# A gated mix of a spectral filter and a Mish MLP on one core: loads of the filter weights moved to GpSimd's queue, the gate row spread by a matmul, another opening and another order of tasks

## The chip, the core and the metric

The kernel runs on one core of a Trainium2 chip. A core has five engines with instruction streams of their own: TensorE (PE; its weight loads are shown apart as PEld), VectorE (DVE), ScalarE (ACT), GpSimd (POOL) and SyncE (SP). They meet only at semaphores. Transfers between the chip's memory (HBM) and the core's SBUF are put into queues by an engine and carried out by 16 DMA engines that all queues share. Matmuls write to PSUM, which has eight banks of 128 x 512 f32.

The metric is device time in microseconds of one execution. The profile is of one such execution; its span is the time from the first to the last recorded instruction, a little under the device time of that execution.

## The reference: what is computed

```python
x = A_x                                          # [1, 2048, 512] bf16
g = sigmoid((x * gate_w).sum(-1, keepdims=True)) # one gate per row of x
# branch A: a filter in the frequency domain
X = rfft2(x, axes=(-2, -1))                      # 2048 x 257 complex
a = irfft2(X * (w_r + 1j * w_i))                 # W = w_r + i w_i: [2048, 257]
# branch B: an MLP on another input name, 512 -> 1792 -> 512, activation Mish
h = x @ w1 + b1
b = (h * tanh(softplus(h))) @ w2
return g * a + (1 - g) * b
```

The kernel as it stands takes x for both branches.

## The kernel before, in words

The 2048 rows of x are 16 tiles of 128 rows; for the MLP four tiles make a chunk (0 to 3).

- MLP, first layer: tasks `m{chunk}_{ft}`, for 14 blocks of 128 hidden columns, four matmuls of 512 columns each (line 847), and ACT's Mish `h{chunk}_{ft}` (line 852) into `hs`. In chunk 0 the blocks 0 to 3 are cut into two halves of two matmuls, `ma0_ft` and `m0_ft`, because w1's first columns come in two transfers, `w1_0_0` and `w1_0_2`. Blocks 8 to 10 need `w1_8_0`. Second layer: `n{tile}_0`, 14 matmuls (line 865), then `o{tile}_0`, which scales by 1 - g.
- The MLP needs x transposed. Tiles 0 to 3 are transposed on PE (`tr0` to `tr3`, line 573) and copied out by `evx0` to `evx3` on ACT or DVE; tiles 4 to 15 by transposing DMAs (`xt4` to `xt15`) in SP's queue, four to a chunk.
- Spectral branch: DVE makes sums and differences of x's halves (`bf`, line 586), PE the stages `p` (line 604), `d` (line 619) and `t0` to `t3` (line 698, with constants `ldM0` to `ldM3`), each followed by a copy out of PSUM (`ep`, `ed`, `et`) on ACT or DVE. Then DVE multiplies by the spectral weights (`hp`, `p1`, `ad`, lines 717 to 724), with a small correction through PE (`e1`, `e2`, then `e3` on DVE, line 767). The way back is `it` (line 780), `id` (line 819) and `ip` (lines 873, 888) on PE.
- The spectral weights W arrive as ten loads into a staging tile `rS` (`wr0s0` and so on, named matrix, half, part; three parts for half 0, two for half 1). DVE and ACT copy them into place: `wrm`/`wim` (lines 646 to 649), the duplicate `wrn`/`win` (line 661).
- The gate: `graw` loads the row `gate_w` copied to all 128 partitions, `gt0` to `gt15` (line 593) on DVE multiply and sum a tile of x with it, `zcl` clips, `ez` (line 681) is a power on POOL, the exponential; from it come `omg` (1 - g), `gc` (g), and, by `ezb`, the PE transpose `zt`, the copy `zte` and the transfers `zw` and `zr` through HBM, a row form of the exponential that `rfs` needs late.

Nothing is scheduled at run time. One string, `ORDER`, lists all tasks; each engine runs its own tasks in that order and stands still until the one at its head has its semaphores, even if a later one could go. A suffix gives the engine and the PSUM bank or slot of `tmp`: `evx2:dve`, `m0_8::7`. Durations written in the code (`pe()`, `dve()`) do nothing at run time.

Three rules of `place` matter. A task that takes a PSUM bank waits for the last users of that bank. A load in SP's queue waits for the landing of the sixth load before it, so that at most six are under way (`KOUT`, lines 268 to 275); this counts only loads in SP's queue. A computing task on POOL waits for the DVE task last marked `lock` ahead of it in the string (lines 261 to 267); DMAs on POOL don't.

The W loads also wait for x, for `cFD` (the constants of `d`) and for w1's first four transfers to land (`deps=t_fr`, line 557). `warm` is matmuls on ones that nobody reads, ahead of the first data; `fl0` and `fl1` are one more each.

Of the kernel before, what the change touches and what calls it, by code (L numbers as in the profile page):

```python
# [8 lines left out]
BF = mybir.dt.bfloat16  # L9
# [6 lines left out]
NFT = 14  # L16
NCH = 4
NF = 64
NFILL = 2
KOUT = 6  # L20
XTP = 4
W1P = ((0, 2, 0, 4), (2, 4, 0, 4), (0, 4, 4, 8), (0, 4, 8, 11), (0, 4, 11, 14))
# [304 lines left out]


ORDER = """
warm::0 fl0::1 fl1::2 ones ident x1 bf1_1 x0 bf0_0 bf0_1 x3 bf3_1 bf3_0 tr1::3 cRF braw evx1:act tr_b::4 x2 bf1_0 w1_0_0 bf2_1 w1_0_2 w1_8_0 ev_b  # L330
bf2_0 tr0::5 tr3::6 p0::0 tr2::7 evx2:dve p1 ep0:dve x4 p2::2 p3 evx3:act w1_4_0 x12 evx0:act ma0_0::4 ma0_2::6 graw::0 ma0_1::5 m0_1 tab w1_11_0 x8
h0_1 m0_2 xt4 xt7 ep2:dve h0_2 xt5 m0_8::7 h0_8 bf4_1 ma0_3::0 bf4_0 m0_3 m0_9::1 h0_9 m0_0 xt6 h0_0 cFD p6::2 h0_3 p7 ep6:dve bf12_0 ldM0 m0_7::5
h0_7 wi0s0 bf12_1 gt12 m0_4::6 h0_4 p4::0 m0_6::7 p5 h0_6 gt14 wi0s2 p14::3 ep4:act m0_10::2 gt13 p12::5 p15 ep14:act ebase m0_5::7 gt5 gt7 h0_10 h0_5
p13 bf8_0 ep12:act bf8_1 gt11 m0_13::0 h0_13 m0_11::1 h0_11 wi0s1 m0_12::3 h0_12 p8::6 p9 ep8:act xt10 gt1 p10::4 p11 ep10:dve m1_9::2 h1_9 wr0s2
m1_12::0 d8::6 d9 xt15 h1_12 xt8 gt8 ed8:act d0::4 d12::2 d13 xt11 ed12:act gt4 xt9 gt9 xt13 gt10 ldM1 wr0s0 m1_4::1 d1 ed0:act wr0s1 d4::6 d5 ed4:act
xt14 m1_13::0 m1_2::2 h1_4 wi1s0 d10::4 d11 ed10:act h1_2 wi1s1 ldM2 d2::6 gt0 d3 m1_8::3 h1_8 m1_5::1 h1_5 gt2 d14::4 gt6 gt15 gt3 zcl d15 ed14:act
wim010:dve m1_3::2 h1_3 ed2:dve m1_10::3 xt12 h1_10 wim011:dve wim000:dve wim001:dve wic0:dve t0::64 d6::1 ez win0:dve h1_13 d7 wr1s0 et00:act
et01:dve wr1s1 m1_0::3 wiz0 hp01_1::1 hp00_1::2 ed6:act m2_2::0 h2_2 hp00_0 h1_0 hp01_0 w2_10 m2_7::6 h2_7 t1::41 et10:act et11:act hp11_0::0 m2_10::7
hp11_1 h2_10 ldM3 m1_1::0 w2_0 m2_5::3 h2_5 wrm000:act m2_0::6 wrm011:dve wrm010:dve ldG2 wrm001:dve wrc0:act c01 m1_7::4 wrn0:dve wrz0 ez1 omg c00
p1_01 m2_9::5 p1_00 m1_6::1 h1_6 h2_0 wim100:dve h1_1 wim101:dve m2_6::2 ad_01 hp10_1::1 m2_3::7 w2_5 ldG0 m2_1::3 h2_1 h2_3 m2_4::1 h2_4 wim111:dve  # L340
m2_11::6 h2_11 hp10_0 h2_6 p1_11 m2_8::0 m1_11::3 h2_8 wim110:dve h2_9 t2::61 et20:act m3_2::0 m2_12::5 m3_6::6 et21:act ad_11 h2_12 m3_1::7 m3_7::1
m2_13::2 p1_10 wic1:act h1_11 wrm111:dve h1_7 wrm101:act wrm100:dve h2_13 m3_12::5 wrm110:dve wrc1:act h3_1 h3_2 m3_0::3 ad_10 wrn1:dve edge ldG1 h3_6
m3_10::4 win1:dve wiz1 ldG3 m3_11::2 h3_11 m3_13::7 h3_0 h3_13 h3_12 wrz1 c02 m3_8::0 hp20_0::0 h3_10 hp20_1 m3_5::6 hp21_0::1 h3_7 m3_9::2 m3_3::3
h3_9 m3_4::7 h3_4 ad_00 hp21_1 p1_21 t3::41 ad_21 et30:act hp30_0::2 n3_0::7 et31:act c03 hp30_1 p1_30 p1_20 h3_3 e1::4 ad_30 xp20::1 h3_8 o3_0:act
ad_20 h3_5 n2_0::5 n0_0::1 xp1::2 xp21 ead::0 e2::2 o0_0:act hp31_1::1 hp31_0 n1_0::3 o1_0:act p1_31 ad_31 rft e3 it5_0::6 it2_0::0 it2_1 it5_1 inv
eit5:act n5_0::4 o5_0:act ezb zt::2 eit2:dve it1_0::0 o2_0:dve it1_1 zte it0_0::6 it0_1 eit0:act zw zr eit1:act it3_0::2 it3_1 eit3:dve n6_0::5
it4_0::6 it4_1 it7_0::3 it7_1 o6_0:dve it6_0::1 it6_1 eit6:act n9_0::0 rfs eit4:dve eit7:act id0::1 id14::6 id15 ec14:act:2 ey14_1 id1 ec0:act:0
id2::4 id3 ec2:act:1 ey0_0 n7_0::3 ey14_0 ey2_0 id10::6 id11 ey2_1 o7_0:act ey0_1 id8::4 id9 ec8:dve:2 ey8_1 id6::1 ec10:act:1 ey10_0 n4_0::3 o4_0:act
ey8_0 ip9_0 ey10_1 id12::4 id7 id13 ec12:dve:0 ey12_1 id4::6 id5 ec4:dve:2 ec6:act:1 n8_0::3 ip8_0 ey6_1 o9_0:act ey6_0 n10_0::0 o8_0:act ey4_0 ip1::1
ey12_0 gc ey4_1 ip5::2 ip4::4 fin4 ip2::5 ip0::3 fin5 ip10_0 fin2 n13_0::6 n14_0::7 ip14_0 ip13_0 out9 n11_0::4 ip11_0 o11_0:act ip6::2 o10_0:dve  # L350
out11 ip7::5 out5 fin1 o14_0:dve fin0 out1 ip3::0 out14 n12_0::1 ip12_0 fin3 n15_0::7 ip15_0 fin6 fin7 o13_0:dve out7 out3 o12_0:dve out13
o15_0:act out15:act
"""


def _build(nc, A_x, A_w_r, A_w_i, B_x, B_w1, B_b1, B_w2, gate_w, out, merge=8, xtp=XTP, NWARM=8):
    cs = _build_consts()
    d_front = nc.inline_tensor(_bf16_bits(cs["front"]), name="c_front").bitcast(BF)
    d_inv = nc.inline_tensor(_bf16_bits(cs["inv"]), name="c_inv").bitcast(BF)
# [7 lines left out]
    with es:  # L367
# [62 lines left out]
        def bank(b, i=0):  # L430
            return ps[:, b.slot + i, :]
# [29 lines left out]
        def dma(name, dst, src, us, cls="dma", queue="sp", is_out=False, transpose=False, grp=None, **kw):  # L461
            def fn(e, _dst=dst, _src=src):
                a = _dst() if callable(_dst) else _dst
                b = _src() if callable(_src) else _src
                if transpose:
                    return e.dma_start(a, b, transpose=True)
                return e.dma_start(a, b)  # L467
# [40 lines left out]


        one = nc.const_aps.tensor(1.0, [128, 128], BF)  # L510
        one2 = nc.const_aps.tensor(1.0, [128, 256], BF)
        wb = _Buf("b1")

        def f_warm(e):
            ins = None
            for _ in range(NWARM):
                ins = e.matmul(bank(wb)[:, 0:256], one, one2, start=True, stop=True)
            return ins

        G.add("warm", [("pe", NWARM * 0.213, f_warm)], "warm", writes=[wb])  # L520
        for k in range(NFILL):
            fb = _Buf("b1")

            def f_fill(e, fb=fb):
                return e.matmul(bank(fb)[:, 0:256], one, one2, start=True, stop=True)
# [21 lines left out]
        for ri, (src, nm) in enumerate(((A_w_r, "wr"), (A_w_i, "wi"))):  # L547
            wv = src.rearrange("(q m) k -> q m k", m=128)
            for fh in range(2):
                sg = stg[64 * ri + 32 * fh:64 * ri + 32 * fh + 32]  # L550
                c0_ = 1 - fh
                parts = [(0, slice(0, 32), slice(32 * fh, 32 * fh + 32), 1.2),
                         (1, slice(c0_, 32), slice(127, 96, -1) if fh == 0 else slice(96, 64, -1), 1.75)]
                if fh == 0:
                    parts.append((1, slice(0, 1), slice(64, 65), 0.1))
                for j, (pm, fs, ms, us) in enumerate(parts):
                    dma(f"{nm}{fh}s{j}", sg[pm:32:2, fs, :], wv[:, ms, :], us, writes=[(nm, fh, "s", j)], deps=t_fr, grp=f"{nm}{fh}")
        for t in range(xtp, NT):
            dma(f"xt{t}", xT[:, t // 4, :, t % 4, :], xv[:, t, :], 0.55, transpose=True, writes=[("xT", t)], grp=f"xt{t // 4}")

# [21 lines left out]
        for a, b_ in XP:  # L582
            w = b_ - a
            for uv in range(2):
                def f_bf(e, a=a, b_=b_, uv=uv):
                    return e.tensor_tensor(out=xu[:, a:b_, uv, :], in0=x_sb[:, a:b_, 0:256], in1=x_sb[:, a:b_, 256:512],  # L586
                                           op=ALU.add if uv == 0 else ALU.subtract)

                t_bf.append(G.add(f"bf{a}_{uv}", [("dve", dve2(256 * w), f_bf)], "bf", lock=True,
                                  reads=[("x", t) for t in range(a, b_)], writes=[("xu", uv, t) for t in range(a, b_)]))  # L590
        t_gt = []
        for t in range(NT):
            t_gt.append(G.add(f"gt{t}", [("dve", 0.6, lambda e, t=t: e.scalar_tensor_tensor(  # L593
# [356 lines left out]
```

## Time and profile before

| | us |
|---|---|
| median of three runs (lowest, highest) | 131.74 (131.31, 131.85) |
| the profiled execution's own time | 131.67 |
| its span | 130.1 |
| PE busy in the span | 124.7 |
| DVE busy | 92.8 |
| ACT busy | 74.0 |
| POOL busy | 4.7 |

A row of a timeline has the start in us, the time from the start to the end of the last one, the engine, the line, the operation, out<-in, the shape, the count, and in brackets the idle time ahead of it with what ended it. Matmuls overlap, so a row of n takes n steps and the length of the last one. SPq and ACTq are the issuing of DMAs, which is not their moving of data; "us to landing" is.

### The profile page before, as it was taken

Reading aid. Unit: us, or ns where it says so; the run is one execution under the profiler, and the core shown is the slowest. Engines: PE = TensorE matmul, PEld = TensorE weight load, DVE = VectorE, ACT = ScalarE, POOL = GpSimd, SP = SyncE. Lnnn points to the kernel's source line nnn. Section 1 sums busy time; section 2 is a strip of 40 time slices with the busy share of each in tenths; the row PEclk is TensorE's granted clock in tenths of the full one; section 3 lists DMA queues with packets and bytes.
Section 4 is the critical chain, followed back from the end, with each engine's and each line's share of the span. In section 5 each row is a group of like instructions: output and inputs, shape, how many; then the busy total and the mean of one; then the engine's idle time right before and its main releaser. Section 6 shows DMA issues by size and latency. Waiting matters only on the chain.

```text
span 130.1 us, 2561 instructions
## 1 busy us (share of the span) xinstructions
PE 124.7 (96%) x1076; PEld 65.2 (50%) x1076; DVE 92.8 (71%) x161; ACT 74.0 (57%) x105; POOL 4.7 (4%) x8
## 2 busy tenths in 40 slices
PE   7969999999999999999999999999999999999991
PEld 4624566665654445444454445556645544444440
DVE  0853797999995899999999996337098692803720
ACT  3852989999999879998959024354432520000202
POOL 2000000000470000000000000000000000000000
PEclk9999999999999999999999999999999999999999
DMA  3889998866799969998400002010000002000591
GB/s 109 247 255 367 316 134 282 126 99 67 198 212 140 262 108 292 363 375 274 166 5 0 0 0 55 0 72 10 5 0 0 5 0 81 0 0 0 187 337 40
DMA packets 17302, 16.88 MB, mean 130 GB/s; under 512 B 7628, under 2 KB 14668, under 8 KB 17228
## 3 DMA queue, kind: packets, MB, share of 16 engines
q1 hardware_dynamic: 17120, 16.60, 51.4%
q8 instruction: 8, 0.13, 0.4%
q10 hardware_dynamic: 172, 0.13, 0.3%
q14 instruction: 2, 0.02, 0.1%
HBM read 13.05 MB, written 2.10 MB: 116 GB/s over the span
## 4 chain that ended last, share of the span: by engine, by line
PE 56%; DVE 28%; ACT 5%; DMA 5%; SPq 2%; issue 2%; DVEq 0%
PE ps L865 28%; PE ps L847 14%; DVE rE L724 8%; DVE tmp L717 6%; DMA w_sb<-in_B_w_dram 5%; DVE rC L720 4%; PE ps L819 3%; PE ps L780 3%; PE ps L619 3%; SPq L467 2%; ACT rC L504 2%; DVE rW L649 2%; PE ps L604 2%; DVE rW L661 2%; PE ps L873 1%
## 5 line engine op out<-in xcount | busy, mean ns | idle before, releaser
L847 PE MATMUL ps<-rX,w_sb 128*128 128x512 bf16 x224 | 50.8, 379 | 1.5 <-DMA w_sb<-in_B_w_dram 1.5
L847 PEld LDWEIGHTS ps<-rX,w_sb 128*128 128x128 bf16 x224 | 21.1, 98 | 25.3 <-DMA w_sb<-in_B_w_dram 2.0
L879 ACT ACTIVATE rX<-ps,omg 128x512 bf16<-128x512 f32 x10 | 6.9, 687 | 37.4 <-PE ps L873 22.6
L865 PE MATMUL ps<-w_sb,hs 128*128 128x512 bf16 x112 | 25.2, 379 | 0.0
L852 ACT ACTIVATE hs<-ps,b1f 128x512 bf16<-128x512 f32 x28 | 18.2, 708 | 4.7 <-PE ps L847 3.6
L865 PEld LDWEIGHTS ps<-w_sb,hs 128*128 128x128 bf16 x112 | 10.5, 98 | 11.9
L865 PE MATMUL ps<-w_sb,rD 128*128 128x512 bf16 x56 | 12.8, 379 | 0.0
L865 PE MATMUL ps<-w_sb,rS 128*128 128x512 bf16 x56 | 12.6, 379 | 0.0
L830 DVE TENSOR_TENSOR rA<-tmp,ps 128x512 bf16<-128x512 f32 x16 | 10.0, 681 | 3.4 <-PE ps L819 3.4
L717 DVE TENSOR_TENSOR tmp<-rC,rA 64x1024 bf16<-64x1024 bf16 x16 | 10.8, 685 | 1.9 <-ACT rC L504 1.4
L504 ACT ACTIVATE rC<-ps 128x1024 bf16<-128x1024 f32 x11 | 11.4, 1060 | 1.0 <-PE ps L698 0.6
L586 DVE TENSOR_TENSOR rB<-rA 128x256 bf16<-128x256 bf16 (+1 forms) x14 | 5.9, 458 | 6.7 <-DMA rA<-in_A_x_dram 6.6
L593 DVE SCALAR_TENSOR_TENSOR rA<-rA,tmp 128x512 bf16<-128x512 bf16 x16 | 10.0, 688 | 0.2
L724 DVE TENSOR_TENSOR rE<-rC,tmp 128x1024 bf16<-128x1024 bf16 x8 | 9.8, 1224 | 0.3
L852 ACT ACTIVATE rD<-ps,b1f 128x512 bf16<-128x512 f32 x14 | 9.0, 692 | 0.9 <-PE ps L847 0.9
L852 ACT ACTIVATE rS<-ps,b1f 128x512 bf16<-128x512 f32 x14 | 8.6, 689 | 1.4 <-PE ps L847 1.4
L892 DVE SCALAR_TENSOR_TENSOR rX<-ps,gcol,rX 128x512 bf16<-128x512 f32 x8 | 5.6, 744 | 5.1 <-PE ps L888 5.1
L865 PEld LDWEIGHTS ps<-w_sb,rS 128*128 128x128 bf16 x56 | 5.5, 98 | 6.6
L882 DVE TENSOR_SCALAR rX<-ps,omg 128x512 bf16<-128x512 f32 x6 | 4.5, 747 | 5.8 <-PE ps L873 4.0
L865 PEld LDWEIGHTS ps<-w_sb,rD 128*128 128x128 bf16 x56 | 5.4, 98 | 6.2
L501 DVE CAST rC<-ps 128x1024 bf16<-128x1024 f32 x5 | 6.0, 1222 | 2.0 <-PE ps L604 2.0
L504 ACT ACTIVATE rF<-ps 128x1024 bf16<-128x1024 f32 x5 | 4.9, 1022 | 3.8 <-PE ps L780 3.8
(77 smaller groups left out, 113.9 us busy)
## 6 DMA issues: line engine op xcount, KB each, us to landing
rF<-c_m SPq DMA_DIRECT2D x4, 512.0 KB, 7.1
rB<-c_g SPq DMA_DIRECT2D x4, 512.0 KB, 7.8
out_dram<-rX SPq DMA_DIRECT2D x7, 256.0 KB, 2.4
rA<-in_A_x_dram SPq DMA_DIRECT2D x3, 512.0 KB, 6.8
w_sb<-in_B_w_dram SPq DMA_DIRECT2D x2, 640.0 KB, 10.3
w_sb<-in_B_w_dram SPq DMA_DIRECT2D x2, 512.0 KB, 8.9
rS<-in_A_w_i_dram SPq DMA_DIRECT2D x3, 257.0 KB, 6.5
rS<-in_A_w_r_dram SPq DMA_DIRECT2D x3, 257.0 KB, 8.4
```

Source lines behind the costliest of these rows:

```text
L501: return e.tensor_copy(out=o(), in_=i())
L504: return e.activation(o(), i(), AF.Copy)
L586: return e.tensor_tensor(out=xu[:, a:b_, uv, :], in0=x_sb[:, a:b_, 0:256], in1=x_sb[:, a:b_, 256:512], op=ALU.add if uv == 0 else ALU.subt ...
L593: t_gt.append(G.add(f"gt{t}", [("dve", 0.6, lambda e, t=t: e.scalar_tensor_tensor(out=x_sb[:, t, :], in0=x_sb[:, t, :], scalar=1.0, in1=tb ...
L717: return e.tensor_tensor(out=z3(z)[lo], in0=y3[hi], in1=wi3[hi], op=ALU.mult)
L724: return e.tensor_tensor(out=Yhq[:, q, h], in0=v(yv), in1=v(tb(z)), op=ALU.add)
L830: return e.tensor_tensor(out=yb[:, t:t + 2, 256 * h:256 * h + 256].rearrange("p t (i e) -> p t i e", e=2), in0=t4(z), in1=o4(bank(b, 1)), ...
L847: ins = e.matmul(bank(b), w1_sb[:, dt_, 128 * ft:128 * (ft + 1)], xT[:, c, dt_, :, :], start=(dt_ == 0), stop=(dt_ == 3))
L852: G.add(f"h{c}_{ft}", [("act", act(512, 1), lambda e, c=c, ft=ft, b=b: e.activation(hs[c][:, ft, :], bank(b), AF.Mish, bias=b1f[:, ft:ft + ...
L865: ins = e.matmul(bank(b)[:, 0:hi - lo], hs[c][:, ft, 128 * tl:128 * (tl + 1)], w2_sb[:, ft, lo:hi], start=(ft == 0), stop=(ft == NFT - 1 a ...
L879: return e.activation(bs[:, t, lo:hi], bank(b)[:, lo:hi], AF.Copy, scale=omg[:, t:t + 1])
L892: return e.scalar_tensor_tensor(out=bs[:, t, :], in0=bank(b), scalar=gcol[:, t:t + 1], in1=bs[:, t, :], op0=ALU.mult, op1=ALU.add)
```

## The change

It has four parts.

1. The ten loads of W are issued from POOL's queue, in the order `wi0s0 wi0s2 wi0s1 wr0s2 wr0s0 wr0s1 wi1s0 wi1s1 wr1s0 wr1s1`, all of them ahead of `ez` on POOL. They still wait for `deps=t_fr`, but no longer count among SP's six.
2. `graw` becomes a load of one row of 512 values into one partition, issued from ACT's queue behind `braw` (the bias). A new PE task `gwm` multiplies a row of ones with it, which copies it to 128 partitions of a PSUM bank, and a new task `gwe` (on ACT) copies that to `tmp`.
3. `warm` is six matmuls of 512 columns instead of eight of 256; `fl0` and `fl1` are gone.
4. `ORDER` is new throughout, with other banks and other choices of engine. On PE the opening is now `tr_b`, `tr1`, `tr0`, `gwm`, `tr3`, `p0`, `tr2`, `p1` to `p3`, and the eight half tasks of blocks 0 to 3 stand ahead of `m0_8`.

```diff
-NFILL = 2
...
 ORDER = """
-warm::0 fl0::1 fl1::2 ones ident x1 bf1_1 x0 bf0_0 bf0_1 x3 bf3_1 bf3_0 tr1::3 cRF braw evx1:act tr_b::4 x2 bf1_0 w1_0_0 bf2_1 w1_0_2 w1_8_0 ev_b
-bf2_0 tr0::5 tr3::6 p0::0 tr2::7 evx2:dve p1 ep0:dve x4 p2::2 p3 evx3:act w1_4_0 x12 evx0:act ma0_0::4 ma0_2::6 graw::0 ma0_1::5 m0_1 tab w1_11_0 x8
-h0_1 m0_2 xt4 xt7 ep2:dve h0_2 xt5 m0_8::7 h0_8 bf4_1 ma0_3::0 bf4_0 m0_3 m0_9::1 h0_9 m0_0 xt6 h0_0 cFD p6::2 h0_3 p7 ep6:dve bf12_0 ldM0 m0_7::5
-h0_7 wi0s0 bf12_1 gt12 m0_4::6 h0_4 p4::0 m0_6::7 p5 h0_6 gt14 wi0s2 p14::3 ep4:act m0_10::2 gt13 p12::5 p15 ep14:act ebase m0_5::7 gt5 gt7 h0_10 h0_5
...
+x1 ebase braw ones ident x0 bf0_0 x3 bf1_0 warm::0 cRF bf1_1 x2 bf0_1 w1_0_0 w1_0_2 w1_8_0 x4 tr_b::1 tr1::2 bf3_1 graw::0 tr0::3 w1_4_0 x12 w1_11_0
+x8 gwm::4 ev_b xt4 evx0:dve tr3::5 bf2_0 p0::6 tr2::0 evx1:act evx2:act gwe:act xt7 bf2_1 evx3:dve xt5 xt6 cFD wi0s0 ldM0 bf3_0 gt3 wi0s2 xt10 tab p1
+xt15 ep0:dve p2::1 p3 ep2:dve ma0_0::3 m0_0 ma0_2::5 m0_2 ma0_3::0 m0_3 h0_3 ma0_1::4 m0_1 h0_1 m0_8::6 wi0s1 h0_2 h0_8 m0_9::7 bf4_0 h0_9 m0_10::1
+h0_10 h0_0 xt8 m0_6::2 h0_6 bf4_1 p6::4 bf12_0 m0_7::0 h0_7 wr0s2 gt7 m0_4::6 h0_4 bf12_1 p4::2 p5 gt5 ep4:act wr0s0 m0_13::7 p14::0 bf8_0 h0_13 p15
+ep14:act p7 ep6:act bf8_1 gt8 wr0s1 gt2 xt11 m0_12::6 wi1s0 h0_12 p12::2 xt9 p13 m0_5::7 h0_5 p8::0 p9 p10::4 gt9 p11 ep8:dve xt13 ldM1 wi1s1 m0_11::6
+m1_0::7 m1_5::0 ep10:act ep12:act d14::4 gt13 d15 gt0 d10::2 h0_11 h1_0 d11 ed10:act m1_4::1 h1_4 xt14 gt1 ed14:dve gt14 h1_5 d6::6 d12::4 ldM2 d13 d7
+ed6:act ed12:dve m1_6::2 xt12 d4::0 gt4 d5 ed4:act m1_10::3 d8::4 gt12 d9 w2_10 ldM3 w2_0 d2::6 gt15 gt6 d3 ed2:dve wr1s0 h1_10 ldG2 gt11 gt10 d0::0
+d1 h1_6 ed0:act m1_8::3 h1_8 m2_4::2 h2_4 wr1s1 t0::06 et01:act m2_13::3 m1_12::2 zcl ez ed8:act m2_2::6 h1_12 m2_0::7 h2_13 wim000:dve wim010:dve
+h2_2 et00:act m1_3::4 h1_3 m2_5::5 t1::20 wim001:dve ezb zt::6 wim011:dve wic0:dve h2_0 et10:act h2_5 ez1 m2_3::4 h2_3 win0:dve zte zw wrm011:dve
+et11:act m2_11::7 h2_11 wiz0 hp10_1::1 m2_7::2 t2::53 et21:act m2_10::0 omg w2_5 m1_11::1 m2_8::7 h2_7 h2_10 et20:act hp10_0 wrm010:dve wim110:dve
...
-def _build(nc, A_x, A_w_r, A_w_i, B_x, B_w1, B_b1, B_w2, gate_w, out, merge=8, xtp=XTP, NWARM=8):
+def _build(nc, A_x, A_w_r, A_w_i, B_x, B_w1, B_b1, B_w2, gate_w, out, merge=8, xtp=XTP, NWARM=6):
...
-        one2 = nc.const_aps.tensor(1.0, [128, 256], BF)
+        one2 = nc.const_aps.tensor(1.0, [128, 512], BF)
...
-                ins = e.matmul(bank(wb)[:, 0:256], one, one2, start=True, stop=True)
+                ins = e.matmul(bank(wb), one, one2, start=True, stop=True)
...
-        for k in range(NFILL):
-            fb = _Buf("b1")
-
-            def f_fill(e, fb=fb):
-                return e.matmul(bank(fb)[:, 0:256], one, one2, start=True, stop=True)
-
-            G.add(f"fl{k}", [("pe", pe(256), f_fill)], "warm", writes=[fb])
...
-        dma("graw", lambda: tb(gwb)[:, 0:512], gate_w.rearrange("(a d) -> a d", a=1).to_broadcast([128, D]), 0.4, writes=[gwb])
+        dma("graw", lambda: tb(gwb)[0:1, 512:1024], gate_w.rearrange("(a d) -> a d", a=1), 0.05, writes=[gwb], queue="act")
...
-                    dma(f"{nm}{fh}s{j}", sg[pm:32:2, fs, :], wv[:, ms, :], us, writes=[(nm, fh, "s", j)], deps=t_fr, grp=f"{nm}{fh}")
+                    dma(f"{nm}{fh}s{j}", sg[pm:32:2, fs, :], wv[:, ms, :], us, writes=[(nm, fh, "s", j)], deps=t_fr, grp=f"{nm}{fh}", queue="pool")
...
+        gb = _Buf("b1")
+        G.add("gwm", [("pe", 0.216, lambda e: e.matmul(bank(gb), one[0:1, :], tb(gwb)[0:1, 512:1024], start=True, stop=True))], "small",
+              reads=[gwb], writes=[gb])
+        evac("gwe", lambda: tb(gwb)[:, 0:512], lambda: bank(gb), 512, [gb], [gwb], "small")
```

In the rest of the order the power's reader `ezb` moves up to DVE's work of that time, `zt` on PE to just behind `t1`, and the stages `t2` and `t3` come earlier; the last tasks on PE are `n15_0` and `ip15_0` in both versions, and the last on ACT `o15_0` and `out15`.

## The prediction

> **What bounds the kernel now.** I read the head of the page first, then the windows view cut where PE's character changes, then PE's timeline, then the queues that feed its opening.
>
> ```profile
> span 130.1 us, 2561 instructions
> PE 124.7 (96%) x1076; PEld 65.2 (50%) x1076; DVE 92.8 (71%) x161; ACT 74.0 (57%) x105; POOL 4.7 (4%) x8
> ```
>
> ```profile
> 0.00:10.05 10.05, 7.39 (x54) 4.35 (x54) 4.66 (x12) 5.72 (x8) 0.69 (x6) 1.00 0.69 209
> 10.05:79.53 69.48, 69.36 (x646) 35.97 (x647) 62.16 (x110) 55.45 (x80) 4.01 (x2) 1.00 0.77 176
> 79.53:127.30 47.77, 47.77 (x377) 24.84 (x377) 25.98 (x39) 12.18 (x17) 0.00 (x0) 1.00 0.14 51
> 127.30:130.10 2.80, 0.16 (x1) 0.00 (x0) 0.00 (x0) 0.69 (x1) 0.00 (x0) 1.00 0.14 47
> ```
>
> In each window's row the second number is its length and the third PE's busy time. From 10.05 to 127.30 PE idles 0.12 us. The last window is the fixed end: the last `o`, its store. What an order can win therefore lies in the first 10.05 us, where PE idles 2.66.
>
> ```profile
> 0.83 1.87 PE L517 MATMUL ps<-const-bfloat16-1.0 128*128 128x256 bf16 x8 [0.83 <-PEq L935]
> 2.49 0.63 PE L525 MATMUL ps<-const-bfloat16-1.0 128*128 128x256 bf16 x2
> 2.99 0.60 PE L573 MATMUL ps<-identt,rA 128*128 128x128 bf16 x4
> 5.03 0.40 PE L573 MATMUL ps<-identt,rA 128*128 128x128 bf16 x4 [0.29 <-DMA rA<-in_A_x_dram]
> 6.19 2.32 PE L847 MATMUL ps<-rX,w_sb 128*128 128x512 bf16 x10
> 10.05 3.19 PE L847 MATMUL ps<-rX,w_sb 128*128 128x512 bf16 x14 [1.54 <-DMA w_sb<-in_B_w_dram]
> 79.53 1.07 PE L780 MATMUL ps<-rB,rE 128*128 128x128 bf16 x16
> ```
>
> Of the 2.66, 0.83 is the start, 0.29 the wait for x2, 1.54 the wait of `m0_8` for `w1_8_0`. Work of PE keeps its amount, so the end moves by what this wait loses, less what is added.
>
> **The change, part by part.** Steps of PE come from the chain of waits:
>
> ```profile
> 80.60 3.02 PE ps L865 x14
> 21.93 0.89 PE ps L604 x16
> 33.73 1.00 PE ps L698 x64
> ```
>
> So 0.2157 us a matmul of 512 columns, 0.0556 one of 128, 1.00 a `t`.
>
> Opening order. Before, ten matmuls stood ahead of `m0_8`; now the eight half tasks, sixteen matmuls, 3.45 us. When can they start? DVE's rows:
>
> ```profile
> 3.44 1.23 DVE L586 TENSOR_TENSOR rB<-rA 128x256 bf16<-128x256 bf16 x5 [0.18 <-DMA rA<-in_A_x_dram]
> 5.00 0.29 DVE L586 TENSOR_TENSOR rB<-rA 128x256 bf16<-128x256 bf16 x1 [0.33 <-DMA rA<-in_A_x_dram]
> 5.49 0.42 DVE L501 COPY rX<-ps 128x512 bf16<-128x512 bf16 x1
> ```
>
> The new DVE order starts at x0 (3.44): five `bf` to 4.65, `ev_b` and `evx0` to 5.2, `bf2_0` and `bf2_1` (x2 landed at 5.00) to 5.7, `evx3` to 6.05, `bf3_0` to 6.3. `p3` waits for that last one, and `ma0_0` stands behind `p3`: about 6.6, that is 0.4 later than now. Sixteen matmuls end at 10.05, where `w1_8_0` lands (its place in SP's queue is the same). The wait is filled exactly, six matmuls more are done by 10.05: 6 x 0.2157 = 1.29 us won. If `ma0_0` starts at 6.2, nothing more is won, as the landing then binds; if at 7.0, 0.9 is left.
>
> Warm-up. Ten matmuls took 0.83 to 2.99, 0.216 each for 256 columns; six of 512 at that rate take 2.6, to 3.4. `tr1` was at 2.99, so it starts 0.4 later; but `p0` waits for `bf0_1` (4.4) and `tr2` for x2 (5.00), so this is covered up to 0.7, beyond which it costs one for one.
>
> `gwm`, `gwe`, `graw`. One matmul, 0.22 (0.43 at the warm-up's rate), stands ahead of `tr3` in the same gap before 5.00; cover as above. It waits for `graw`, now behind `braw` on ACT:
>
> ```profile
> 0.80 0.65 ACTq L467 DMA_DIRECT2D rD<-in_B_b_dram  x1
> tmp<-in_gate_w_dram SPq DMA_DIRECT2D x1, 128.0 KB, 8.1
> rA<-in_A_x_dram SPq DMA_DIRECT2D x4, 128.0 KB, 2.2
> ```
>
> Issued by 2.1, at a small load's 2.2 it lands at 4.3. Bounds: 1.3 (the shortest landing in the trace, the `scz` store below) to 8.1, what the broadcast took behind a full queue; at 8.1 all behind `gwm` would move 4 us. I take 2.2, since ACT's queue has nothing before it but 3.5 KB. `gwe` is one ACT copy of some 0.55 ahead of the Mish table; ACT's first Mish waits for `m0_3` at 8.3 anyway.
>
> ```profile
> scz<-rD SPq DMA_DIRECT2D x1, 4.0 KB, 1.3
> ```
>
> SP. It loses eleven issues, and the six-load rule counts other loads. In the rows, the last is the transposes' time from issue to landing.
>
> ```profile
> 11.32 5.34 SPq L466 DMA_TRANSPOSE rX<-in_A_x_dram  x4
> 16.70 0.58 SPq L467 DMA_DIRECT2D rD<-c_front  x1
> 20.67 1.94 SPq L467 DMA_DIRECT2D rS<-in_A_w_i_dram  x3
> 24.63 7.81 SPq L466 DMA_TRANSPOSE rX<-in_A_x_dram  x5
> rD<-c_front SPq DMA_DIRECT2D x1, 128.0 KB, 3.9
> DMA to landing us min/median/max: 2.7/4.8/9.6
> ```
>
> `xt4` now waits for `w1_8_0` (10.05) instead of x4 (11.3): transposes, `cFD` and all behind move up 1.3, and `cFD` lands at 19.3 instead of 20.6. Chunk 1 is needed at 10.05 + 11.3 (10 m of 0.863, 12 `p` of 0.223) = 21.4, its last transpose is issued by 15.4, lands near 20.2. Chunk 2's fourth (`xt9`) is issued at about 23, lands near 28, wanted by `m2_4` at 10.05 + 20.0 = 30.1. The longest landing of a transpose was 9.6, which would be 32.6.
>
> POOL. Ten loads, from `cFD` at 19.3 on, then `ez`.
>
> ```profile
> L467 SPq DMA_DIRECT2D rS<-in_A_w_i_dram x5: 581/616/644, 20.7 to 36.3; - x5
> rS<-in_A_w_i_dram SPq DMA_DIRECT2D x3, 257.0 KB, 6.5
> rS<-in_A_w_r_dram SPq DMA_DIRECT2D x3, 257.0 KB, 8.4
> 34.28 3.90 POOL L681 TENSOR_TENSOR ezs<-ebase,zcl 128x16 f32<-128x16 f32 x1 [17.89 <-DVE rA L667]
> 30.57 1.23 DVE L501 CAST rE<-ps 128x1024 bf16<-128x1024 f32 x1
> 31.83 0.70 DVE L649 TENSOR_SCALAR rA<-rS 32x2064 bf16<-32x2064 bf16 x1
> L593 DVE SCALAR_TENSOR_TENSOR rA<-rA,tmp 128x512 bf16<-128x512 bf16 x16 | 10.0, 688 | 0.2
> ```
>
> No row shows a load issued by POOL. Bounds for one: 0.6, the same load on SP, to 3.9, POOL's one long instruction. I take 1.2, near SP's costliest issue (a transpose, 5.34 for four): POOL is done at 31.3. DVE reaches `zcl` then: `d3` ends at 10.05 + 18.7 (15 m, 12 `p`, 14 `d`) = 28.8, `ed2` (1.23) and two `gt` (10.0 for sixteen, 0.63 each) follow, `zcl` ends near 31.7. `ez` runs to 35.6. DVE is at `ezb` at 33.9, after three copies of W of 0.70, and waits 1.7; but four small tasks on, `hp10_1` waits for `et10`, whose `t1` ends at 38.1, so this wait costs about nothing. PE's next stop is `zt`, at 10.05 + 28.1 (23 m, 28 `p` and `d`, 2 `t`) = 38.1. So POOL has 38.1 - 0.3 - 3.9 - 19.3 = 14.6 us for ten issues: 1.46 each is free. W's data have more room: the last pair lands by 31.3 + 8.4 = 39.7, read at about 47.
>
> By the Trainium skill, "DMA: Bandwidth & Descriptors", section Specifications, a load issued by GpSimd has its first byte after about 1 us against 0.6 from SP; an estimate from it would be 1.0 an issue and the same sum. No run here shows it yet.
>
> DVE's middle. From 36.84 to 79.03 DVE goes from the first `hp` to `e3`, 42.2 with a wait of 1.45. The new order has a duplicate (an L661 row) and two copies of W less there and an `o` more.
>
> ```profile
> 36.84 2.61 DVE L717 TENSOR_TENSOR tmp<-rC,rA 64x1024 bf16<-64x1024 bf16 x4
> 40.90 1.40 DVE L717 TENSOR_TENSOR tmp<-rC,rA 64x1024 bf16<-64x1024 bf16 x2 [1.45 <-ACT rC L504]
> 44.84 1.24 DVE L661 TENSOR_SCALAR rW<-rW 64x4160 bf16<-64x4160 bf16 x1 [0.38 <-ACT rW L668]
> 79.03 0.44 DVE L767 CAST rE<-ps 128x64 bf16<-128x64 f32 x1
> ```
>
> That is 42.2 - 1.45 - 1.24 - 1.40 + 0.7 = 38.8; from 39.4 on, `e3` comes at 78.2, or 79.7 with a wait as long as now; PE wants it at 10.05 + 69.6 + 0.8 (the drift of now: 69.48 against 68.7 by counts) = 80.4. It holds with about a microsecond to spare, and every further wait of DVE's beyond that is PE's.
>
> Sum: -1.29 (opening) + 0 (warm-up, `gwm`, in the gap before x2) + 0 (POOL) + 0 (tail, the same last tasks). The profiled execution is 131.67, 0.07 under the median of 131.74, and 1.57 above its span. 131.67 - 1.29 = 130.4.
>
> **Rivals.** *POOL issues slowly.* PE stops at `zt`, in order, for 10 x (pace - 1.46); at 1.59 the gain is gone, at 2.0 the stop is 5.4 and the time 130.4 + 5.4 = 135.8; SP would stand at `zw` with `w2_5` behind it. For it: POOL's instructions are slow here (3.9 for 128 x 16). Against: until `zcl` nothing else is on POOL.
>
> The Trainium skill ("SBUF — State Buffer", section "SBUF: two separate sides") says that while DVE runs a two-port operation GpSimd can't write descriptors. In this trace `ez` overlaps a DVE copy and takes 3.90, which agrees but proves nothing. By that rule issues left after 31.7 would meet three copies of 0.70, and the pace at which the gain is gone falls from 1.59 to 1.38.
>
> *Transposes late.* W's loads now run beside the transposes instead of taking turns with them in one queue. If `xt9` lands as late as the longest row, PE stands 2.5 at `m2_4`: 132.9. Against: SP is far ahead of its former place (`xt9` was the fourth of the five issued from 24.63 to 32.44).
>
> *Nothing comes of it.* `graw` or the copies delay `ma0_0` to 7.5 and beyond, or a bank in the new order binds for a microsecond: 131.3 to 132.0.
>
> **How the numbers follow.** Under 0.5% (0.66 us), about what a measurement of this kernel can tell from no change, counts as the same. Forecast, 130.4 with its own range 129.7 to 131.0: 0.48. Slow POOL, 132.4 to 137: 0.24. Late transposes or another new stop in the middle, 132.4 to 134: 0.12. Nothing: 0.16. The range runs from 129.6 (the 0.29 at x2 and a shorter end won too) to 135.0, which leaves out about 0.05 below and 0.12 above.
>
> **What will show it.** Right: PE's wait for w1 ahead of line 843 under 0.4 us; sixteen matmuls ahead of it; POOL's last load before 32; `ezs` over by 36; no PE idle at the transpose of `ezb`. Wrong: DVE or PE waiting for `ezs`, PE waiting for `rX` transposes, or the first line 843 matmul after 7.

## The result, and the profile after

The changed kernel takes 139.22 us (median of six executions, 138.0 to 146.06); the kernel before, on the same chip, takes 131.59 (131.25 to 131.85). The ratio is 1.055, 95% interval 1.051 to 1.060: slower by 5.5%, where 130.4 was forecast and 135.0 was the end of the range. The ratios of this document leave out executions more than 1.5% above the quickest of their kernel; here these are 146.06 and the one profiled, 143.67, in which the granted clock was lowest (0.953 and 0.964, against 0.974 to 0.986).

The head of the page, with the granted clock and the DMA engines in 40 slices of 3.56 us:

```profile
span 142.4 us, 2546 instructions
...
PE   7999999950029999999999999999999999999992
...
PEclk9999999999555999999999999999999999999999
DMA  3899999993999936200060000063000000121145
```

PE has one hole, in slices 9 to 12, and its clock is at 5 tenths in slices 11 to 13, that is in the hole and just behind it. PE's timeline around the opening and the hole:

```profile
6.62 7.25 PE L843 MATMUL ps<-rX,w_sb 128*128 128x512 bf16 x31
13.70 0.39 PE L600 MATMUL ps<-rD,rB 128*128 128x128 bf16 x4
...
29.70 0.81 PE L843 MATMUL ps<-rX,w_sb 128*128 128x512 bf16 x3
41.75 1.89 PE L843 MATMUL ps<-rX,w_sb 128*128 128x512 bf16 x4 [11.23 <-DMA rX<-in_A_x_dram]
43.57 1.89 PE L694 MATMUL ps<-rE,rF 32*128 32x128 bf16 x64
45.79 5.22 PE L843 MATMUL ps<-rX,w_sb 128*128 128x512 bf16 x23 [0.33 <-issue]
```

The stop is at `m2_4`, the first block of chunk 2 (line 843 is what line 847 was, 694 what 698 was). It was ready at 30.5 and waited 11.23 us for the transposes of chunk 2. Its four matmuls then take 1.82 to the next start instead of 0.86, and the `t` behind them 1.89 instead of 1.00, since the clock is halved. So 11.23 + 0.96 + 0.89 + 0.17 (the longer issue gap at 45.79) = 13.25 us; 130.4 + 13.25 is the 143.67 of this execution. By the spans (130.1 - 1.29 + 13.25 = 142.06 against 142.4) 0.3 us is left over; no other wait of PE behind the opening is longer than 0.2 us.

Now the loads. SP's and POOL's issuing:

```profile
17.33 8.58 SPq L465 DMA_TRANSPOSE rX<-in_A_x_dram  x6
```

```profile
20.27 1.83 POOL L466 DMA_DIRECT2D rS<-in_A_w_i_dram  x3 [18.75 <-DMA rD<-c_front]
22.10 1.63 POOL L466 DMA_DIRECT2D rS<-in_A_w_r_dram  x3
23.72 1.15 POOL L466 DMA_DIRECT2D rS<-in_A_w_i_dram  x2
24.86 1.13 POOL L466 DMA_DIRECT2D rS<-in_A_w_r_dram  x2
32.33 3.38 POOL L677 TENSOR_TENSOR ezs<-ebase,zcl 128x16 f32<-128x16 f32 x1 [6.35 <-DVE zcl L675]
```

The six transposes are the four of chunk 2 and two of chunk 3. `xt9`, chunk 2's last, is the fifth: it was issued at about 23, and chunk 2 was complete only at 41.7. POOL issues ten loads in 5.7 us, 0.57 each, and is done at 26.0. From issue to landing (KB each, median us):

```profile
rF<-c_m SPq DMA_DIRECT2D x4, 512.0 KB, 10.2
rS<-in_A_w_i_dram POOLq DMA_DIRECT2D x3, 257.0 KB, 13.1
rS<-in_A_w_r_dram POOLq DMA_DIRECT2D x3, 257.0 KB, 15.8
...
rX<-in_A_x_dram SPq DMA_TRANSPOSE x12, 6.7
```

W took 6.5 and 8.4 before, a transpose 4.8. What the 16 DMA engines did from 24 to 40 us, by queue (packets, MB, share of their time), in the kernel before:

```profile
q1 hardware_dynamic: 4949, 2.43, 92.0%
```

and in the changed kernel, q0 being POOL's queue and q1 SP's:

```profile
q0 software_dynamic: 413, 1.75, 85.7%
q1 hardware_dynamic: 1255, 0.31, 21.4%
```

Before, the engines were nearly full (92%; the shares add up packets' times, and can pass 100 together), with some room from 28 to 34 us: 0.41, 0.82 and 0.39 in windows of 2 us. In the changed kernel they were full. W has 86% of them, and everything that SP issued, chunk 2 among it, gets 0.31 MB through in 16 us.

How dear W's bytes are shows over the whole execution of the changed kernel:

```profile
q1 hardware_dynamic: 14704, 14.36, 36.2%
q0 software_dynamic: 512, 2.11, 10.8%
```

W's 2.11 MB take 10.8% of 142.4 us, that is 15.4 us of all sixteen engines, or 7.3 us a MB; SP's 14.36 MB take 51.5 us, 3.6 a MB. W is dear from SP's queue as well: in the kernel before its packets, the only ones of 514 and 16,448 bytes, took 12.3 us of all sixteen.

### The profile page after: what moved, and what is told of

It is laid out like the page before. It is cut to its first block, busy times and chain, and to the rows that moved or that the text cites. A ratio compares the mean times of both kernels' runs of the same rounds, so it can differ in the third digit from the quotient of the medians.

```text
span 142.4 us, 2546 instructions
## 1 busy us (share of the span) xinstructions
PE 125.8 (88%) x1057; PEld 65.6 (46%) x1073; DVE 93.1 (65%) x163; ACT 79.4 (56%) x104; POOL 9.9 (7%) x18
## 3 DMA queue, kind: packets, MB, share of 16 engines
q1 hardware_dynamic: 14704, 14.36, 36.2%
q0 software_dynamic: 512, 2.11, 10.8%
## 4 chain that ended last, share of the span: by engine, by line
PE 36%; DVE 26%; DMA 22%; SPq 11%; issue 3%; ACT 0%; DVEq 0%
PE ps L861 21%; DMA rX<-in_A_x_dram 13%; DVE tmp L713 8%; SPq L465 6%; DVE rE L720 6%; PE ps L843 6%; DMA w_sb<-in_B_w_dram 5%; SPq L466 4%; DVE rC L716 4%; DMA rB<-c_g 4%; PE ps L815 3%; PE ps L694 2%; DVE rW L645 2%; PE ps L776 2%; DVE rW L644 1%
## 5 line engine op out<-in xcount | busy, mean ns | idle before, releaser
L843 PE MATMUL ps<-rX,w_sb 128*128 128x512 bf16 x212 | 50.8, 384 | 12.5 <-DMA rX<-in_A_x_dram 11.2
L843 PEld LDWEIGHTS ps<-rX,w_sb 128*128 128x128 bf16 x224 | 21.0, 99 | 35.6 <-DMA rX<-in_A_x_dram 11.7
L503 ACT ACTIVATE rC<-ps 128x1024 bf16<-128x1024 f32 x13 | 13.5, 1074 | 1.9 <-PE ps L694 1.9
L848 ACT ACTIVATE rS<-ps,b1f 128x512 bf16<-128x512 f32 x14 | 9.1, 686 | 1.1 <-PE ps L843 1.1
L503 ACT ACTIVATE rF<-ps 128x1024 bf16<-128x1024 f32 x4 | 4.0, 1022 | 3.4 <-PE ps L776 3.3
## 6 DMA issues: line engine op xcount, KB each, us to landing
rS<-in_A_w_i_dram POOLq DMA_DIRECT2D x3, 257.0 KB, 13.1
rS<-in_A_w_r_dram POOLq DMA_DIRECT2D x3, 257.0 KB, 15.8
```

The costliest lines, as they stand in the source:

```text
L503: return e.activation(o(), i(), AF.Copy)
L843: ins = e.matmul(bank(b), w1_sb[:, dt_, 128 * ft:128 * (ft + 1)], xT[:, c, dt_, :, :], start=(dt_ == 0), stop=(dt_ == 3))
L848: G.add(f"h{c}_{ft}", [("act", act(512, 1), lambda e, c=c, ft=ft, b=b: e.activation(hs[c][:, ft, :], bank(b), AF.Mish, bias=b1f[:, ft:ft + ...
```

## The experiments

The theory after the first look: between 17 and 45 us the DMA engines are the limit, and W takes them from chunk 2. The rivals: the new order alone asks for chunk 2 too early, whatever W does; or a transpose in SP's queue is slow by itself. The expectations give these theories names: AMOUNT, SHARING and SUPPLY for versions of the first, MIXING for W and transposes holding each other up, ORDER and SP ALONE for the rivals. "Before" on the same chips was 131.6 to 132.0.

**The changed kernel again (`after_copy`).** No edit.

> The changed kernel again, as the yardstick of the others. 138 to 140 us; line 843's matmuls stand 7 to 11 us for the transposes of chunk 2 (tile rX), the granted clock falls to half within that stop. Theories, for all runs that follow. MIXING: W's loads, coming from a second queue, share the DMA engines with the transposing loads, and the two kinds hold each other up, so both crawl although little is moved. AMOUNT: the six-load limit no longer holds W back, and there is simply too much under way for the engines. ORDER: the new order of SP's own loads makes the transposes late, whichever queue W uses.

Measured: 140.99 (137.89 to 143.49). PE's wait in its profile:

```profile
39.36 1.89 PE L843 MATMUL ps<-rX,w_sb 128*128 128x512 bf16 x4 [7.37 <-DMA rX<-in_A_x_dram]
```

The stop is there again at the same block. Its length differs, 7.4 against 11.2: how the queues meet is not the same in two executions.

**W back in SP's queue, the new order kept (`after_sp`).**

```diff
-..., deps=t_fr, grp=f"{nm}{fh}", queue="pool")
+..., deps=t_fr, grp=f"{nm}{fh}")
```

> The changed kernel with W's ten loads back in SP's queue (at the same places of the order, again counted among the six). MIXING and AMOUNT: no stop for chunk 2 above 1 us, 130.3 to 131.0, since the opening's gain of 1.1 to 1.3 us stays. ORDER: the stop stays, 134 or more.

Measured: 139.28 (138.32 to 139.69), ratio 1.0545 [1.0493, 1.0598]. The 130.3 to 131.0 that two of the theories gave is missed; the stop stays, as ORDER said. PE, and SP's queue around it:

```profile
36.79 1.89 PE L843 MATMUL ps<-rX,w_sb 128*128 128x512 bf16 x4 [6.08 <-DMA rX<-in_A_x_dram]
```

```profile
17.13 0.58 SPq L466 DMA_DIRECT2D rD<-c_front  x1
20.90 0.62 SPq L466 DMA_DIRECT2D rS<-in_A_w_i_dram  x1
...
32.38 2.58 SPq L465 DMA_TRANSPOSE rX<-in_A_x_dram  x2
```

Here the cause is in the open: W's first load waits for `cFD` at the head of SP's queue (17.7 to 20.9), W stands between the transposes, and chunk 2's last, `xt9`, is the first of the two issued from 32.4 on. So part of this stop is late issue. But compare with the changed kernel: there `xt9` was the fifth of six issued by 25.9, some nine microseconds earlier, and chunk 2 landed five microseconds later (41.7 against 36.8; 39.4 in the copy). An earlier issue bought nothing.

**The kernel before with W in POOL's queue, and nothing else (`before_pool`).**

```diff
-... deps=t_fr, grp=f"{nm}{fh}")
+... deps=t_fr, grp=f"{nm}{fh}", queue="pool")
```

> The kernel before with this one part of the change: W's ten loads from POOL's queue. MIXING and AMOUNT: the transposes of chunk 2, wanted at about 35.9, land late; line 847 stands 3 us or more for rX; 134 to 141. ORDER: no such stop, 131.0 to 132.5.

Measured: 138.7 (134.99 to 139.35, four executions); the quickest is still 3.0 us above the 132.02 of the kernel before on that chip. PE in the execution of 139.35:

```profile
40.61 2.54 PE L847 MATMUL ps<-rX,w_sb 128*128 128x512 bf16 x8 [4.23 <-DMA rX<-in_A_x_dram]
43.98 1.90 PE L698 MATMUL ps<-rE,rF 32*128 32x128 bf16 x64 [0.83 <-ACT rD L852]
```

In the old order too, which wants chunk 2 at 36.4, W on POOL makes chunk 2 late, and the clock is halved behind the stop (granted clock 1.00 up to 41.7, 0.50 from there to 48.5). So each part does it by itself: the new order with W on SP 139.3, the old order with W on POOL 138.7, both together 139 to 141. The two don't add up. That they draw on one shortage would explain it; these runs alone don't show it. Nor do they show which does the harm in POOL's queue, the second queue or the missing limit of six: no run has the one without the other.

**W withheld until chunk 2 has landed (`pool_after_xt2`)**, and **until all twelve transposes have (`pool_after_xt`)**.

```diff
-..., deps=t_fr, grp=f"{nm}{fh}", queue="pool")
+..., deps=t_fr + [t_xt[t] for t in range(8, 12)], grp=f"{nm}{fh}", queue="pool")
```

(with `range(4, 16)` in the second, and W's tasks moved behind `xt9` and `xt12` in `ORDER`)

> The changed kernel, W still from POOL, but each of its loads waits until the four transposes of chunk 2 have landed. MIXING and AMOUNT: those four land by 30, the stop at m2_4 is under 1 us, W comes some 8 us later than planned, which DVE feels at its first copy of W by 0 to 4 us: 130.5 to 135. ORDER: chunk 2 still lands after 35.

> The changed kernel, W from POOL only after all twelve transposes have landed: a measurement of W by itself beside plain loads. MIXING: the ten loads land in under 10 us from the first issue, since no transpose is about. SHARING, AMOUNT: some 13 us or more again, since W's short rows set the pace. Time 136 to 142, as W comes late to DVE and the power is issued behind it.

Measured: the first 138.68 (135.7 to 143.59; ratio 1.0288 [1.0237, 1.0339]), the second 141.95, one execution. The first misses its 130.5 to 135, its quickest execution by 0.7. Rows of that execution: POOL, then DVE.

```profile
27.92 1.84 POOL L466 DMA_DIRECT2D rS<-in_A_w_i_dram  x3 [26.39 <-DMA rX<-in_A_x_dram]
```

```profile
37.61 0.70 DVE L645 COPY rA<-rS 32x2064 bf16<-32x2064 bf16 x1 [5.08 <-DMA rS<-in_A_w_i_dram]
```

With W out of the way chunk 2 has landed by 27.9, before it is wanted, and `m2_4` doesn't stop. This is what W was costing it: 39 to 42 against 28. But now W is late, and DVE's copies wait for it; PE stops 1.20 us, up to 40.0, for `ezb`, which stands among them, and 2.07 us ahead of `t2`, up to 45.0, for nothing that the profile shows. In the second kernel, W's landings, with no transpose under way any more:

```profile
rS<-in_A_w_i_dram POOLq DMA_DIRECT2D x3, 257.0 KB, 10.8
rS<-in_A_w_r_dram POOLq DMA_DIRECT2D x3, 257.0 KB, 12.7
```

MIXING had all ten loads landed in under 10 us there, and missed: W is slow without any transpose beside it. It needs no company at all. From 42 to 48 us SP's queue moves 13 packets and next to no bytes, and POOL's 1.12 MB still take 103% of the engines' time, 187 GB/s. So it is not the meeting with transposes that is dear; W's loads hold the engines long by themselves.

**Chunk 2 wanted 8 us later (`after_late2`, W on POOL; `after_sp_late2`, W on SP).** Eight blocks of chunk 1 change places with chunk 2's first eight.

```diff
-... m2_4::2 h2_4 wr1s1 t0::06 et01:act m2_13::3 m1_12::2 ...
+... m1_12::2 h1_12 wr1s1 t0::06 et01:act m1_3::3 m1_11::2 ...
```

> The changed kernel, W from POOL, with the same exchange of blocks. SHARING (W from a second queue takes its part of the engines at once, and chunk 2 lands at 39 to 42 though its loads go out earlier): a stop of 0 to 2.5 us is left, 130.5 to 133. MIXING (W and transposes in two queues slow the engines as such): the same stop, but under 150 GB/s from 20 to 42 us, where the kernel before has 156.

> The changed kernel with W back in SP's queue, and with eight of chunk 1's blocks done where the new order has chunk 2's first eight, so that PE asks for chunk 2 at about 39 instead of 30.7; nothing else differs. ORDER, read anew (the new order asks for chunk 2 before the DMA engines can bring it, at 36.8 here): the stop for rX goes, 130.5 to 132, or up to 134 if W's last loads, now last in the queue, come late to DVE. If the stop had another cause (the banks, ACT), it stays above 3 us.

Measured: with W on POOL 134.44 (133.59 to 139.26), ratio 1.0191 [1.014, 1.0242]; with W on SP 139.11 (137.41 to 139.89), ratio 1.0484 [1.0416, 1.0551]. The stop for `rX` is gone in both, as expected, and both times are missed (up to 133, and up to 134). MIXING's own sign, under 150 GB/s from 20 to 42 us, came out at 149 and decides nothing. Both profiled executions (139.26 and 139.61) stop at the next thing. PE with W on POOL:

```profile
43.57 1.90 PE L694 MATMUL ps<-rE,rF 32*128 32x128 bf16 x64 [5.66 <-DMA rF<-c_m]
```

and with W on SP, PE and DVE:

```profile
41.33 1.20 PE L694 MATMUL ps<-rE,rF 32*128 32x128 bf16 x64 [3.57 <-DMA rF<-c_m]
```

```profile
56.38 0.70 DVE L645 TENSOR_SCALAR rW<-rS 32x2064 bf16<-32x2064 bf16 x1 [5.64 <-DMA rS<-in_A_w_r_dram]
```

`t1` waits for its constants `ldM1`, which SP issued behind the transposes, or W's last half is late. The wait moves from load to load.

**M's loads ahead of chunk 3's transposes as well (`after_late2_m`).** As `after_late2`, and in SP's queue (the loads alone, the tasks between them left out):

```diff
-xt10 xt15 xt8 xt11 xt9 xt13 ldM1 xt14 ldM2 xt12
+xt10 ldM1 xt8 xt11 xt9 ldM2 xt15 xt13 xt14 xt12
```

> The changed kernel with the eight blocks of chunk 1 exchanged ahead of chunk 2's first eight (134.4 us, its stop at t1 for ldM1 5.7 us), and with ldM1 and ldM2 issued ahead of chunk 3's transposes, ldM1 behind the first of chunk 2's. SUPPLY: the stop at t1 goes, and since the same bytes are moved something else is late by what the engines lack: chunk 2 at about 40 or W's last loads at about 50; less than 4 us stay lost in all, 131.0 to 134.0. ORDER OF THE LOADS ONLY (nothing lacks; each load was only in the wrong place): no stop over 0.5 us before 60 us and 130.0 to 130.9.

Measured: 134.97 (131.86 to 137.93, four executions). Both expectations are missed. In the profiled execution, 137.93, PE no longer waits for any load, and yet it stops inside `t1`, after 21 of its 64 matmuls:

```profile
37.63 0.50 PE L694 MATMUL ps<-rE,rF 32*128 32x128 bf16 x21
42.85 1.36 PE L694 MATMUL ps<-rE,rF 32*128 32x128 bf16 x43 [4.71 <-issue]
```

"Issue" means that PE waited for nothing that the profile shows. The queue of instruction loads has eight packets of 16 KB in each execution. In the kernel before the second of them stands in the window from 29 to 32 us:

```profile
q8 instruction: 1, 0.02, 2.6%
```

In this kernel the queue q8 moves nothing in all of 20 to 40 us, while W and SP's loads have the engines:

```profile
q0 software_dynamic: 314, 1.18, 62.9%
q1 hardware_dynamic: 2496, 1.68, 45.6%
```

The packet comes in the window from 40 to 42.5:

```profile
q8 instruction: 1, 0.02, 2.9%
```

PE goes on at 42.85. So what ran out may well have been PE's own instructions, whose load came ten microseconds late through the same engines. The stop of 2.07 us in `pool_after_xt2` is of this kind too: it ended at 45.0, and a packet of q8 stands between 43.5 and 45.5 there. The times fit; the profile doesn't say whose instructions a packet holds, and no run here tests it by itself. The execution at 131.86 would be one in which it came in time, but it has no profile.

**W's bytes taken away, all else as in the changed kernel (`after_small_w`).**

```diff
-dma(f"{nm}{fh}s{j}", sg[pm:32:2, fs, :], wv[:, ms, :], ...
+dma(f"{nm}{fh}s{j}", sg[pm:32:2, fs, :][:, 0:(1 if j == 2 else 4)], wv[:, ms, :][:, 0:(1 if j == 2 else 4)], ...
+G.add("zW", [("pool", 6.0, lambda e: e.memset(rS[:], 0.0))], ...)
```

> The changed kernel with W's ten loads on POOL as they are, but each moving only the first 4 of its 31 or 32 rows to a partition (0.28 MB in place of 2.1 MB; the rest of the staging tile is set to zero once by POOL before 12 us, so the output is not the reference's). SUPPLY (from 17 to 45 us the 16 DMA engines are the limit, and W's bytes are what makes chunk 2's transposes and t1's constants late): the stop of m2_4 for rX, 7 to 11 us in the changed kernel, goes or is under 1.5 us; t1 does not stop for c_m by more than 1 us; transposes land in a median under 5.5 us; the time is 130.0 to 132.0, what the prediction gave for the whole change. SP ALONE (the transposes are late because SP issues them late or their rows are slow, whatever W does): the stop stays at 4 us or more and the time at 134 or more.

This kernel leaves out seven eighths of W, so its output is not the reference's; the computing is that of the changed kernel, and a `memset` on POOL, over by 8.6 us, comes on top.

Measured: 130.31 (130.05 to 132.28, five executions), ratio 0.9884 [0.9842, 0.9925]. That is the forecast of 130.4 to 0.1 us, where the interval leaves 129.7 to 130.8. The profiled execution is the one of 132.28, whose opening ran slower (32 matmuls from 7.63 to 15.95); in the middle, PE and the same 16 us of the DMA queues:

```profile
31.55 1.89 PE L845 MATMUL ps<-rX,w_sb 128*128 128x512 bf16 x8
33.37 1.07 PE L696 MATMUL ps<-rE,rF 32*128 32x128 bf16 x64
34.37 5.35 PE L845 MATMUL ps<-rX,w_sb 128*128 128x512 bf16 x24
39.66 1.07 PE L696 MATMUL ps<-rE,rF 32*128 32x128 bf16 x64
```

```profile
q1 hardware_dynamic: 4608, 3.43, 89.1%
q0 software_dynamic: 289, 0.25, 11.1%
```

No stop anywhere, same order, same queues, same ten issues. SP's queue moves 3.43 MB in the 16 us in which it moved 0.31 beside the whole of W. SUPPLY's numbers are met (130.0 to 132.0; transposes landed in a median of 4.6), and SP ALONE's (134 or more) are not: what the change lost, it lost through W's 1.8 MB at that time. The engines are no less full here, 89% and 11%, but with bytes that are wanted then: 233 GB/s from 20 to 42 us, where the changed kernel has 147 and the kernel before 156. The edit makes W's packets smaller as well as fewer (0.28 MB in 320, instead of 2.11 MB in 512), so the two are not told apart.

**The opening alone, in the kernel before (`before_open`, `before_open2`, `before_open3`).** The first moves `ma0_3 m0_3 m0_0` ahead of `m0_8`; the second also `m0_10` ahead of `p6`; the third is the second with other banks and `m0_5` ahead of `p12`. The third's edit:

```diff
-... m0_8::7 h0_8 bf4_1 ma0_3::0 bf4_0 m0_3 m0_9::1 h0_9 m0_0 ... p6::2 ... m0_7::5 ... m0_4::6 ... m0_6::7 ... m0_10::2 ...
+... ma0_3::0 m0_3 m0_0 m0_8::7 h0_8 bf4_1 bf4_0 m0_9::1 h0_9 ... m0_10::5 h0_10 p6::2 ... m0_7::6 ... m0_4::7 ... m0_6::5 ...
```

> The kernel before with one thing of the new order alone: the second halves of blocks 0 and 3 and the first half of block 3 go ahead of m0_8, so that sixteen matmuls stand before it instead of ten. The forecast's term for the opening: the wait for w1_8_0 goes from 1.54 us to under 0.4, span 128.8 to 129.3, ratio 0.990 to 0.994. If the wait only moves (to the next load of w1, or to the end), 0.997 to 1.003.

> The kernel before, with ma0_3, m0_3 and m0_0 ahead of m0_8 and also m0_10 (whose w1 has landed) ahead of p6, with banks 5 and 3 for m0_10 and m0_7. If what was left of the opening's wait is only x4 (landed at 11.3) ahead of p6, as before_open had it with 0.75 us: that wait goes too, t0 starts at 32.4 to 32.7 in place of 33.3, and the time is 130.4 to 130.9 against the kernel before, 0.6 to 1.0 per cent faster. If chunk 2's transposes, landed just before they were wanted at 36.4, bind then: a wait of 0.5 us or more ahead of chunk 2's first block and 131.2 or more.

> As before_open2, with banks chosen so that m0_7, m0_4 and m0_6 wait for no copy (6, 7 and 5) and m0_5 ahead of p12. If the opening's gain is there to be had without touching W or the order behind it: no wait of PE over 0.3 us between 6 and 33 us, t0 at 32.4 to 32.7 (33.7 in the kernel before, 33.3 in before_open), and 130.5 to 131.0 us, 0.5 to 0.9 per cent faster than the kernel before. If the loads in the middle take it back, as they took the changed kernel's: a wait for rX, c_m or rS of 0.5 us or more appears behind 33 us and the time is 131.2 or more.

Measured: 131.36, ratio 0.9988 [0.9957, 1.0018]; 132.13, ratio 1.0021 [0.9998, 1.0043]; 131.28 (130.73 to 132.28), ratio 0.9987 [0.9959, 1.0015]. PE in the three:

```profile
12.66 0.62 PE L604 MATMUL ps<-rD,rB 128*128 128x128 bf16 x8 [0.75 <-DVE rB L586]
```

```profile
14.56 1.90 PE L847 MATMUL ps<-rX,w_sb 128*128 128x512 bf16 x8 [1.32 <-DVE rC L501]
```

```profile
6.58 1.46 PE L847 MATMUL ps<-rX,w_sb 128*128 128x512 bf16 x6 [0.25 <-DMA w_sb<-in_B_w_dram]
8.39 4.70 PE L847 MATMUL ps<-rX,w_sb 128*128 128x512 bf16 x21 [0.35 <-DMA w_sb<-in_B_w_dram]
...
32.90 1.07 PE L698 MATMUL ps<-rE,rF 32*128 32x128 bf16 x64
```

In the first the wait for `w1_8_0` becomes one of `p6` for DVE's `bf4`, which itself starts when x4 has landed, at 11.3. In the second that is gone, and I had put `m0_7` into a bank that `p6` takes with its neighbour, so it waits for a copy. In the third `t0` starts at 32.90 instead of 33.7, 0.8 us earlier (0.2 less than expected, for two short waits for w1), and the profiled execution is 130.92; but over twelve executions the gain is 0.1 to 0.3% and can't be told from none. That misses the 130.5 to 131.0, and without the wait behind 33 us that was the other outcome; where the 0.8 us went in the other executions is open. No version here with the reference's result is measurably faster than the kernel before.

## Why the prediction was wrong

- *Opening order*: right in the trace. Sixteen matmuls and more run from 6.62 (6.6 forecast) without a stop, and `p6`, behind 32 of them, comes at 13.70 where 6.6 + 32 x 0.2157 gives 13.50. The 1.29 us fit `after_small_w`, which gains 1.45 in all (by its interval 1.0 to 2.1); by itself the opening showed 0.8 us in the trace of `before_open3` and no measurable gain in time.
- *Warm-up*; *`gwm`, `gwe`, `graw`*: right, at no cost. With W small no wait of PE for any of them shows.
- *POOL*: the result right, the pace not. An issue took 0.57 us, below the lower bound of 0.6 and half of the 1.2 taken; `cFD` landed at 20.3, not 19.3. `ezs` was over at 35.7 (35.6 forecast), by luck so near: `ez` began 0.6 later than forecast, when `zcl` ended, and took 3.38 instead of 3.9. The rival "POOL issues slowly" falls; so does the estimate of 1.0 an issue from the Trainium skill's "DMA: Bandwidth & Descriptors", Specifications, whose figure is for the first byte and not for the pace of issue. All ten issues were over by 26.0, ahead of DVE's first copy of W at 32.2, so the part of that rival on DVE's copies went untested. The fast pace put W on the engines by 26 instead of 31, where the transposes had to share them.
- *SP*: this step failed. "Lands near 28" was the time of issue plus about 5, the time to landing read from the kernel before. There W, the transposes and M took turns in one queue, at most six at a time. With W in a queue of its own `xt9`, issued at about 23 as forecast, took 18.5 us instead of 5 and landed at 41.7. "SP is far ahead of its former place" was true, and no protection: place in SP's queue counts only against what else is in SP's queue.
- The same mistake stands in *POOL*: the last pair of W was put at its issue plus 8.4. W's loads of 257 KB took 13.1 and 15.8 (medians).
- *DVE's middle*: could not be seen in the changed kernel. With W small no stop of PE stands at `e3` or behind.
- The rival "Transposes late" had the right place and the right mechanism, but 2.5 us, from the longest landing of the kernel before (9.6). It was 7.4 and 11.2 in the two profiles, and about 2 more for the halved clock, which no step priced. It also had too small a chance, 0.12.

What I missed was in the profile of before: the kernel's DMA engines are at six to nine tenths in every slice of the page from 16 to 62 us, and at 92% by their packets' times from 24 to 40. With so little room a move of 2.1 MB, 15 us of all the engines as they measured, to an earlier time can't leave the other loads' times alone. The order before asks for chunk 2 at 36.0 and for the constants of `t2` at 51.0, and issues W's last two loads at 40.3; the new one asks for chunk 2 at 30.5, for the constants of `t2` at 43.5 (in `after_small_w`), and has issued all of W by 26.0. The engines didn't deliver that.

Why W, of all, wins over SP's loads may show in the window from 35 to 40 us of the changed kernel:

```profile
q0 software_dynamic: 163, 0.69, 82.0%
q1 hardware_dynamic: 171, 0.04, 18.2%
```

About one packet of SP's goes for each of POOL's, but POOL's take 0.40 us each on average (82.0% of 16 x 5 us over 163), SP's 0.085. The Trainium skill says this as a rule ("DMA: Bandwidth & Descriptors", section "Queues, rings and completion order"): each DMA engine goes round its queues and takes a whole packet from one before it turns to the next. The trace agrees here, 163 to 171; over the longer window from 24 to 40 it is 413 to 1255, which shows no such turn-taking; there not all engines may have had W all the time. With that rule, the queue whose packets take longer gets more of the engines' time. The records of single packets in the traces fit: W's rows of 514 bytes go as 2048 packets of 0.056 us from SP's queue in the kernel before, and mostly as 224 packets of 4112 bytes and 0.42 us from POOL's; and ten packets of 16,448 bytes that POOL's queue began between 31.1 and 31.3 us took 4.0 to 4.5 us each. No run changed the size of the packets alone, so this share of the explanation is argued; that W's loads are the cause is shown, since the stop goes when their bytes are left out (`after_small_w`) and when they wait for chunk 2 (`pool_after_xt2`).

Of the halved clock the Trainium skill has a rule too ("TensorE: Matmul & The Clock Gate", section "HAM oscillation — how this bites in real kernels"): an idle gap over some 3.4 us halves it. The traces agree in part: after 11.23, 7.37 and 6.08 us of stop the next rows run at half speed, and after 4.23 (`before_pool`) the clock halves 1.1 us behind the stop. But in `pool_after_xt2` it is at 0.50 from 45.4 to 48.8 too, behind stops of only 1.20 and 2.07 us, so a gap of that length is not needed.

## What to carry to other kernels

The time from issue to landing is not a property of the load alone but of what else is on the DMA engines (a transpose's median was 4.8 us before, 6.7 and 8.6 with W in POOL's queue, 4.6 with W small): before a load is moved ahead, or to a queue of its own, add up the engines' share in the windows it moves into, in time and not in bytes, and if they are full, say which other load will come later instead. A limit on loads under way, or one queue for all, may look like a nuisance and yet hold other loads' landings in place. The quickest test is to leave the bytes out and keep everything else.

## What was not expected of the hardware

- POOL issued W's ten loads in 5.7 us, 0.57 each, no slower than SP's 0.6.
- In the middle of a kernel instructions are loaded through the same DMA engines, eight packets of 16 KB in each execution. One that came at 40 instead of 30 us goes with a stop of PE of 4.7 us that the profile puts down to "issue".
- W's loads on POOL keep their 11 to 13 us even when no transpose is under way, and hold the engines full at 187 GB/s when nothing else moves (`pool_after_xt`).
